# VectorE's share of the softmax exponentials: a 16-bit log word used three times in place of a log word and its parabola

## The chip, the core and the metric

The kernel runs on one core of one Trainium2 chip. The time is the device time of one launch in microseconds (us). The engines are PE (TensorE: PE rows are matmuls, PEld rows are weight loads), ACT (ScalarE), DVE (VectorE), POOL (GpSimd) and SP, which here only issues DMAs.

## The reference

Two transformer layers over one sequence of 2048 tokens of width 512, in bfloat16. Each layer is attention with 32 heads of width 16, then a ReLU feed-forward of width 1792; both sit behind a layer norm and add to x. The same weights serve both layers.

```python
def _A_ref(x, wqkv, wo):
    B, S, D = x.shape                      # 1, 2048, 512
    H = 32
    Dh = D // H                            # 16
    qkv = (x @ wqkv).reshape(B, S, 3, H, Dh) ...   # q, k, v by head
    scores = jnp.einsum("bhqd,bhkd->bhqk", q, k) * (Dh ** -0.5)
    p = _softmax(scores, axis=-1)
    o = jnp.einsum("bhqk,bhkd->bhqd", p, v)
    return (...o...).reshape(B, S, D) @ wo

def _B_ref(x, w1, w2):
    h = jnp.einsum("bsd,df->bsf", x, w1)
    h = jnp.maximum(h, zero)
    return jnp.einsum("bsf,fd->bsd", h, w2)

x = A_x
x = x + _A_ref(_layernorm(x), A_wqkv, A_wo);  x = x + _B_ref(_layernorm(x), B_w1, B_w2)
x = x + _A_ref(_layernorm(x), A_wqkv, A_wo);  x = x + _B_ref(_layernorm(x), B_w1, B_w2)
```

The attention scores are 2 x 32 x 2048 x 2048 numbers, and each needs an exponential. They never leave the core: scores are made in PSUM, an exponential of them is written to SBUF, and that is the moving operand of the product with the values.

## The kernel before

**Slots.** The scores are worked off in 1366 slots. A slot has three blocks of 128 keys x 512 queries (each in one PSUM bank; late in the kernel a block is cut into pieces 256 or 128 queries wide, of several key blocks). There are two sets of three banks, `ps_s0` and `ps_s1`, used in turn. In a slot PE makes the scores with 32-row tiles (line 1497, called S here), ACT takes `exp` of them into one of five buffers `e` (line 1506), and later PE multiplies `e` by the values `vaug` into `ps_o`, four 32-column tiles at a time (line 1077, a value round, V). `vaug` carries a column of ones, so that the softmax's denominator comes out of the same product. S of a slot can start when the exponentials of the slot two before it have been read out of the same bank set.

**VectorE's blocks.** In many slots the third block goes to DVE, and ACT's instruction is then 1024 wide in place of 1536. DVE turns the scores of its block into an int16 number in units of 1/128 octave (line 1184, `lin`): read as bfloat16, the bits of that number are a first approximation of 2^x that is linear between powers of two. Three blocks of such slots make a group (`GROUP = 3`), and when the third one's number is there, `chain` (the lines 1228, 1237 and 1240) works on the 128 x 1536 group:

- `square` gets the mantissa of `lin`, by a bitwise AND and OR (line 1228);
- in groups where the values are not held in a scaled copy `vscaled` (keys 7 to 11), `square` is multiplied by a constant (line 1237);
- `square` is multiplied by `lin`, both read as bfloat16: the parabola (line 1240, the only operation with two tensors);
- `lin` is cut to its exponent by AND and OR, in place (line 1228).

PE then adds two products per block to `ps_o`, `square` x values and `lin` x values. There are four `lin` buffers (`NP`) and three `square` buffers (`NC`).

**The filler.** Everything else, the projections, the output projection, the feed-forward and the transposes, is cut into pieces of matmuls that go into `ps_f` (line 480, called F here) and are put into the gaps of PE between S and V. Their results are read out of PSUM by DVE.

**The order.** There is no dynamic schedule. The program is written by a planner in Python, run at build time: it keeps its own clocks of PE, DVE and ACT (`now_pe`, `now_dve`, `exp_end`) with fixed costs (`MM` 216 ns for a round of matmuls, `SWITCH` 105 ns for a change between S and V or F), and decides with them, slot by slot, which block DVE takes, which pieces and value rounds go in front of the next S, and when the steps of `chain` stand in DVE's order. If PE has time to spare in a slot, S is issued again to keep PE busy (`times`, the loop ahead of line 1497). Whether a slot may begin a new group for DVE is decided in the condition with `pair_no[0] + 1 - pairs[0]["n"] < NP`: there must be a free `lin` buffer, and the group's queued work (`CHAIN`) must end before its segment of keys does. On the chip each engine then runs its list in that order and waits on semaphores.

After the last slot follows a tail, in which the last rows pass through output projection, layer norm and feed-forward on PE, ACT and DVE by turns.

Of the kernel before, what the change touches and what calls it, by code (L numbers as in the profile page):

```python
# [25 lines left out]
def kernel(  # L26
# [10 lines left out]
    nc = tc.nc  # L37
    P = 128
# [24 lines left out]

    SQUARE, SUM = 0.99278, 1.0 / 0.66857
    LOG2E = 1.4426950408889634
    UNIT = 128.0
    EXP_BIAS = (127.0 - math.log2(SUM)) * UNIT
    GROUP = 3  # L70
    CHAIN = 2500.0
    FILL = 4000.0
    SOON = 1500.0
    NP = 4
    NC = 3
    SCALED = (7, 8, 9, 10, 11)

    MM = 216.0
# [21 lines left out]
    FULL = 3  # L100
    LOOK = 3
    NORM_UNITS = 12.0

    ctx.enter_context(tc.manual_schedule())
    persist = ctx.enter_context(tc.tile_pool(name="persist", bufs=1))
# [2 lines left out]
    def sb(shape, dt, name):  # L108
        return persist.tile(shape, dt, name=name)
# [37 lines left out]
    ot = [sb([P, QS], BF16, f"ot{T}") for T in range(NT // 2)]  # L147
    ot_last = sb([P, P], BF16, "ot_last")
    lin = [sb([P, GROUP * QS], I16, f"lin{n}") for n in range(NP)]
    square = [sb([P, GROUP * QS], BF16, f"square{n}") for n in range(NC)]  # L150

    acc = [
        x[:].bitcast(FP32).rearrange("p a b -> p (a b)") for x in kt01 + kt2
# [128 lines left out]
    def mark(key, engine="dve", lag=0.0):  # L282
        made[key] = (engine, (now_pe if engine == "pe" else now_dve)[0] + lag)
# [141 lines left out]
    def run_until(key):  # L425

        if key in made:
            return
        finish_group()
        if key in made:  # L430
            return
        if key not in maker:
            kind, l, j = key[1]
            for i in range(chunks[l, j][1]):
# [261 lines left out]
    def scale_v(l, kb, deps):  # L696
        task(
            225, lambda: nc.vector.tensor_scalar(
                out=vscaled[kb][:], in0=vaug[l][kb][:], scalar1=SQUARE, scalar2=None, op0=ALU.mult
            ),  # L700
            [("third", l, kb)], [("v", l, kb)] + deps,
        )
# [370 lines left out]
    def pv(sg, kb, g, rhs, p=None):  # L1073
        e = sg["e"]
        values = vscaled[kb] if p and p["scaled"] else vaug[sg["l"]][kb]
        sg["rem"][g] -= 1
        nc.tensor.matmul(  # L1077
            ps_o[32 * g : 32 * g + 32, 0 : sg["w"]],
            values[:, 4 * sg["T"] + g, 2 * e : 2 * e + 32],
            rhs, start=g not in sg["begun"], stop=not sg["rem"][g],  # L1080
            tile_position=(0, 32 * g), skip_group_check=True,
        )
        sg["begun"].add(g)
# [31 lines left out]
    def v_round(found, t):  # L1115
        pe_run("v", 1, t)
        sg = segs[seg_at[0]]
        for n in range(QS // sg["w"]):
            for g in range(4):
                of_g = [f for f in found if f[1][2] == g][n : n + 1]  # L1120
                for home, x, rhs in of_g:
                    home[:] = [y for y in home if y is not x]
                    pv(sg, x[1], g, rhs, *x[5:])
        while pend and not pend[0]["blocks"]:
            pend.popleft()
        for p in [p for p in pairs if len(p["blocks"]) == GROUP and not p["mms"]]:
            pairs.remove(p)
            mark(("added", p["n"]), "pe")
        if not any(sg["rem"]):
            finish_segment(sg, sg is segs[-1])  # L1130
            seg_at[0] += 1
# [40 lines left out]
        v_round(found, t)  # L1172


    pairs = deque()
    pair_no = [0]
    step1_end = {}
# [2 lines left out]
    def dve_block(half, taken, src, ex, recent):  # L1180
        which = (pair_no[0] + (half == 0)) % NP

        def first_step():
            first = nc.vector.tensor_scalar(  # L1184
                out=lin[which][:, half * QS : (half + 1) * QS], in0=src, scalar1=EXP_BIAS,
                scalar2=0.0, op0=ALU.add, op1=ALU.max,
            )
# [12 lines left out]

        if half == 0:
            pair_no[0] += 1
            pairs.append({"sg": taken[0][0], "key": ("e", pair_no[0]), "n": pair_no[0], "blocks": [], "mms": [], "scaled": False})
        p = pairs[-1]
        p["blocks"].append(taken)
        for sg, kb, g in taken:
            sg["rem"][g] += 1
        line_key = ("line", p["n"], half)
        p["mms"] += [
            (sg, kb, g, part[:, half * QS + n * sg["w"] : half * QS + (n + 1) * sg["w"]], key) + of  # L1210
            for part, key, of in (
                (square[p["n"] % NC], p["key"] + ("square",), (p,)),
                (lin[which][:].bitcast(BF16), p["key"], ()),
            )
            for n, (sg, kb, g) in enumerate(taken)
        ]
        p["mms"].sort(key=lambda x: len(x[4]), reverse=True)
        musts.append((EVAC, now_pe[0] + PE_TO_DVE, first_step))

    def chain(p):  # L1220
        key, n = p["key"], p["n"]
        line, power = lin[n % NP][:], square[n % NC][:]
# [4 lines left out]
        def bits(out, keep, put):  # L1227
            nc.vector.tensor_scalar(  # L1228
                out=out, in0=line, scalar1=keep, scalar2=put, op0=ALU.bitwise_and,
                op1=ALU.bitwise_or,  # L1230
            )

        half_mantissa = power if p["scaled"] else power.bitcast(FP16)
        quick = 77 + 0.2588 * GROUP * QS
        steps = [(quick, ("half",), lambda: bits(power.bitcast(I16), 0x7F, 0x3F00))]
        if not p["scaled"]:
            steps.append((quick, ("weighed",), lambda: nc.vector.tensor_scalar(
                out=half_mantissa, in0=power, scalar1=SQUARE, scalar2=None, op0=ALU.mult)))
        steps += [
            (77 + 0.52 * GROUP * QS, ("square",), lambda: nc.vector.tensor_mul(  # L1240
                out=power, in0=half_mantissa, in1=line.bitcast(BF16))),
            (quick, (), lambda: bits(line, 0x7F80, 0)),
        ]
        after = [("added", n - NC)] if n > NC else []
        for cost, of, fn in steps:
            task(cost, fn, [key + of], after)
            maker[key + of]["chain"] = p
            after = [key + of]

    for n in range(NW1):  # L1250
        load_w1(n)
# [109 lines left out]
    now_dve[0] = 14500.0  # L1361
    exp_end = {-1: 12600.0, 0: 13600.0}
    pair_at = None
    def in_turn(x):
        sg, kb, g = x[1]
        return sg["n"], sg["e"], kb % (QS // sg["w"])

    while units:
# [21 lines left out]
        half = None  # L1390
        if len(banked) == W and (pair_at is None or no > pair_at or now_dve[0] < now_pe[0] + SOON):
            mine = banked[-1][0][0]
            if pair_at is not None:
                half, take = len(pairs[-1]["blocks"]), pairs[-1]["sg"]
            elif (not pairs or pair_no[0] + 1 - pairs[0]["n"] < NP) and ((mine['l'] or ("v", 0, 15) in made or len(pairs) < 3 and ("v", 0, 5) in made or not pairs and ("k", 0, 0, 1) in made) and (not mine['l'] or ('k', 1, 0, NQS - 1) in made or pace < PAIR_PACE)):
# [79 lines left out]
        s_ready = max(exp_end[no - 2] + ACT_TO_PE, step1_end.get(no - 2, 0.0) + DVE_TO_PE)  # L1475
        need_by = exp_end[no - 1] - MM - PE_TO_ACT
        limit = max(need_by - 60.0, s_ready) - SWITCH
        late = len(pend) >= 3
        for kind in ("v", "f", "v") if late else ("f", "v", "f"):
            if kind == "f":  # L1480
                fill_pe(limit)
            else:
                fill_v(limit, 3)

        spare = int(max(need_by - pe_start("s", s_ready), 0.0) / MM)
        soon = (len(pend) > 1) + (owed[0] > 1.0 and (bool(cur) or not evac))
# [213 lines left out]
```

## Time and profile before

| | us |
|---|---|
| median of 3 runs | 1526.84 (1523.2 to 1528.97) |
| profiled execution, its own time | 1527.95 |
| span of its instructions | 1526.2 |
| from the span's start to the first `exp` of a slot | 14.62 |
| from there to the end of the last one | 1485.40 |
| from there to the end (the tail) | 26.2 |
| ACT busy | 1483.9 (97%) |
| DVE busy | 1427.3 (94%) |
| PE busy / weight loads busy | 1383.3 (91%) / 525.3 (34%) |

In a row of groups stand the line, the engine, the operation, output <- input by their names, the shapes, the count, then busy time in us and the mean duration of one in ns, then the engine's idle time before such instructions and what ended it. On every engine a record begins before the one ahead of it has ended (the records of two neighbours overlap by 70 to 270 ns), so the mean duration is more than an instruction costs in a row of its kind; the distance from start to start is what it costs.

### The profile page before, as it was taken

What the parts mean: (1) busy time and instruction counts of PE and PEld (TensorE: products, weight loads), DVE (VectorE), ACT (ScalarE), POOL (GpSimd) and SP (SyncE); (2) the same over time, 40 slices, a digit from 0 to 9 for tenths busy, and PEclk for the clock granted to TensorE, in tenths of its full rate; (3) what the DMA queues carried; (4) which work ended last, traced back from release to release, by engine and by line L of the source; (5) the groups of instructions that cost most, each with busy time, mean ns of one, the idle gap of its engine ahead of it and who ended that gap; (6) DMA issues with size and microseconds to landing.
All of it is one profiled execution on the core that took longest, in us unless ns stands there. A gap on an engine that the chain in (4) does not pass through costs nothing.

```text
span 1526.2 us, 45694 instructions
## 1 busy us (share of the span) xinstructions
PE 1383.3 (91%) x19996; PEld 525.3 (34%) x20000; DVE 1427.3 (94%) x2474; ACT 1483.9 (97%) x1393; POOL 104.7 (7%) x244
## 2 busy tenths in 40 slices
PE   8889888998999998999889998888999999999998
PEld 3222222232232222333223232222234444445665
DVE  7889999999999999999799998789999999999984
ACT  7989999999999999999999999999999999999994
POOL 4000001001010011000110001001001000010100
PEclk9999999999999999999999999899999999999999
DMA  7000000111002010120101100000110111121221
GB/s 197 19 5 23 20 13 15 42 25 22 17 20 45 18 23 13 23 50 20 23 5 29 29 5 5 6 18 8 43 41 19 36 31 29 36 52 44 62 55 28
DMA packets 135144, 46.32 MB, mean 30 GB/s; under 512 B 119808, under 2 KB 132160, under 8 KB 134944
## 3 DMA queue, kind: packets, MB, share of 16 engines
q1 hardware_dynamic: 128032, 37.34, 10.5%
q0 software_dynamic: 5568, 5.15, 1.9%
q8 instruction: 156, 2.56, 0.7%
q10 hardware_dynamic: 1344, 0.92, 0.2%
q14 instruction: 44, 0.36, 0.1%
HBM read 24.38 MB, written 2.10 MB: 17 GB/s over the span
## 4 chain that ended last, share of the span: by engine, by line
ACT 73%; PE 11%; DVE 11%; issue 2%; DMA 2%; POOL 1%; SPq 1%; DVEq 0%; ACTq 0%
ACT e L1506 73%; PE ps_s L1497 4%; DVE lin L1184 4%; PE ps_o L1077 3%; PE ps_f L480 3%; DVE square L1240 1%; DVE ht L794 1%; DVE square L1228 1%; DMA w<-in_B_w_dram 1%; PE ps_s L1560 1%; DVE lin L1228 1%; DMA wv<-in_A_wqkv_dram 0%; PE ps_s L480 0%; DVE vaug L706 0%; SPq L221 0%
## 5 line engine op out<-in xcount | busy, mean ns | idle before, releaser
L1506 ACT ACTIVATE e<-ps_s 128x1024 bf16<-128x1024 f32 (+1 forms) x1366 | 1471.3, 1320 | 14.8 <-PE ps_s L1497 9.7
L1497 PE MATMUL ps_s<-q,ktp 32*128 32x512 bf16 (+2 forms) x6605 | 610.3, 328 | 104.3 <-ACT e L1506 88.1
L1184 DVE TENSOR_SCALAR lin<-ps_s 128x512 int16<-128x512 f32 x861 | 578.4, 685 | 31.0 <-PE ps_s L1497 23.4
L1077 PE MATMUL ps_o<-e,vaug 128*32 128x512 bf16 (+2 forms) x4450 | 436.3, 329 | 9.8 <-DVE vaug L706 1.5
L1497 PEld LDWEIGHTS <-ktp 32*128 32x128 bf16 x6605 | 217.0, 92 | 553.8 <-issue 336.8
L1240 DVE TENSOR_TENSOR square<-square,lin 128x1536 bf16<-128x1536 bf16 (+1 forms) x287 | 270.1, 947 | 0.2
L1077 PEld LDWEIGHTS <-vaug 128*32 128x32 bf16 x5800 | 155.3, 94 | 269.8 <-issue 243.9
L480 PE MATMUL ps_f<-xnT,w 128*32 128x512 bf16 (+2 forms) x2048 | 153.6, 344 | 6.3 <-DVE ht L794 3.3
L1228 DVE TENSOR_SCALAR lin<-lin 128x1536 int16<-128x1536 int16 x287 | 157.3, 549 | 0.2
L1228 DVE TENSOR_SCALAR square<-lin 128x1536 int16<-128x1536 int16 x287 | 153.4, 552 | 0.3
L480 PE MATMUL ps_f<-w,ht 128*32 128x512 bf16 x1624 | 145.0, 381 | 0.8 <-DVE xn L738 0.3
L1077 PE MATMUL ps_o<-lin,vaug 128*32 128x512 bf16 (+2 forms) x1182 | 133.3, 326 | 0.9 <-DVE lin L1228 0.9
L1077 PE MATMUL ps_o<-square,vscaled 128*32 128x512 bf16 (+2 forms) x1014 | 115.3, 329 | 1.1 <-DVE r L975 0.7
L480 PE MATMUL ps_f<-xnT,wkq 128*32 128x512 bf16 (+2 forms) x1376 | 108.4, 352 | 4.8 <-DVE x L833 1.2
L794 DVE TENSOR_SCALAR ht<-ps_f 128x512 bf16<-128x512 f32 x105 | 71.7, 683 | 1.5 <-PE ps_f L480 1.2
L480 PEld LDWEIGHTS <-w 128*32 128x32 bf16 x2080 | 55.3, 96 | 36.7 <-issue 23.2
L480 PEld LDWEIGHTS <-ht 128*32 128x32 bf16 x1680 | 45.1, 96 | 28.9 <-issue 14.4
L526 POOL TENSOR_TENSOR ta<-stats 128x4 f32<-128x4 f32 (+2 forms) x17 | 7.0, 409 | 592.1 <-DVE stats L517 592.1
L480 PE MATMUL ps_f<-wo,ot 128*32 128x512 bf16 x496 | 45.1, 382 | 1.7 <-DVE vaug L706 1.0
L480 PEld LDWEIGHTS <-wkq 128*32 128x32 bf16 x1376 | 35.5, 95 | 30.5 <-issue 20.2
L517 DVE BATCH_NORM_STATS2 stats<-x 128x6 f32<-128x512 bf16 x64 | 42.9, 684 | 2.1 <-DMA x<-in_A_x_dram 1.2
L1077 PEld LDWEIGHTS <-vscaled 128*32 128x32 bf16 x1014 | 35.5, 95 | 26.7 <-issue 24.5
(142 smaller groups left out, 577.0 us busy)
## 6 DMA issues: line engine op xcount, KB each, us to landing
w<-in_B_w_dram SPq DMA_DIRECT2D x130, 128.0 KB
q<-xn SPq DMA_DIRECT2D x44, 64.0 KB
out_dram<-x SPq DMA_DIRECT2D x16, 128.0 KB
x<-in_A_x_dram SPq DMA_DIRECT2D x14, 128.0 KB
w<-in_B_w_dram SPq DMA_DIRECT2D x1, 1792.0 KB
u<-r POOLq DMA_DIRECT2D x12, 128.0 KB, 4.5
ktp<-in_B_w_dram SPq DMA_DIRECT2D x10, 128.0 KB
u<-ht POOLq DMA_DIRECT2D x6, 128.0 KB, 4.5
```

Source lines behind the costliest of these rows:

```text
L480: nc.tensor.matmul(out[cols], lhsT[:, cols], rhs, start=i % k == 0, stop=i % k == k - 1, tile_position=(0, 32 * g), skip_group_check=True,)
L517: nc.vector.bn_stats(out=stats[ln_n(tag)][:, i, :], in_=x_t[tt][:])
L526: pool.tensor_tensor(out=t1, in0=st[:, :, 1], in1=st[:, :, 4], op=ALU.subtract)
L794: nc.vector.tensor_scalar(out=out, in0=sums, scalar1=0.0, scalar2=None, op0=ALU.max)
L1077: nc.tensor.matmul(ps_o[32 * g : 32 * g + 32, 0 : sg["w"]], values[:, 4 * sg["T"] + g, 2 * e : 2 * e + 32], rhs, start=g not in sg["begun" ...
L1184: first = nc.vector.tensor_scalar(out=lin[which][:, half * QS : (half + 1) * QS], in0=src, scalar1=EXP_BIAS, scalar2=0.0, op0=ALU.add, op1 ...
L1228: nc.vector.tensor_scalar(out=out, in0=line, scalar1=keep, scalar2=put, op0=ALU.bitwise_and, op1=ALU.bitwise_or,)
L1240: (77 + 0.52 * GROUP * QS, ("square",), lambda: nc.vector.tensor_mul(out=power, in0=half_mantissa, in1=line.bitcast(BF16))),
L1497: nc.tensor.matmul(b[:, a : a + sg["w"]], kt[32 * g : 32 * g + 32, kc : kc + P], qbuf[sg["n"] % 2][32 * g : 32 * g + 32, sg["e"], 0 : sg[" ...
L1506: ex = nc.scalar.activation(out=eb[:, 0 : place[m]], in_=b[:, 0 : place[m]], func=ACTF.Exp, scale=1.0 / (LOG2E * UNIT),)
L1560: uses(nc.tensor.matmul(out, lhsT, rhs, start=first, stop=last), b, needs=needs)
```

## The change

The parabola goes. The number `lin` stays as it is for its whole life and is used three times: read as bfloat16 itself, and as two copies, `up` with 41 added and `down` with 41 taken off (41/128 of an octave), each not below 0. Each copy is one `tensor_scalar` with add and max on int16 (line 1243 of the changed kernel). In groups whose values have no scaled copy `down` is multiplied by a constant (line 1248). PE adds three products per block in place of two: `lin`, `up` and `down`. The first can go as soon as a block's `lin` is there; before, both waited for the group's steps.

The buffers are two each of `up` and `down` in place of three of `square`. The planner is told when each part's products are done (`("free", part, n)`), a new group needs a `lin` buffer that is free in that sense (`lin_free`), and some of its constants change (`CHAIN` 2500 to 1500; no new group where the filler's pace is above `MOST`, except in some early slots; value rounds with four columns filled are preferred unless three or more slots wait). One line asks for another layer's chunk table in `run_until`, and `vscaled` carries `WEIGHT` in place of `SQUARE`.

```diff
-    SQUARE, SUM = 0.99278, 1.0 / 0.66857
+    THIRD, WEIGHT, SUM = 41.0, 1.55, 3.63198
-    CHAIN = 2500.0
+    CHAIN = 1500.0
-    NC = 3
+    NC = 2
+    MOST = 4.0
...
-    square = [sb([P, GROUP * QS], BF16, f"square{n}") for n in range(NC)]
+    up = [sb([P, GROUP * QS], I16, f"up{n}") for n in range(NC)]
+    down = [sb([P, GROUP * QS], I16, f"down{n}") for n in range(NC)]
...
     # in dve_block
-            sg["rem"][g] += 1
+            sg["rem"][g] += len(PARTS) - 1
...
-            for part, key, of in (
-                (square[p["n"] % NC], p["key"] + ("square",), (p,)),
-                (lin[which][:].bitcast(BF16), p["key"], ()),
+            for part, buf, key, of in (
+                ("lin", lin[which], line_key, None),
+                ("up", up[p["n"] % NC], p["key"] + ("up",), None),
+                ("down", down[p["n"] % NC], p["key"] + ("down",), p),
...
     # in chain
-        half_mantissa = power if p["scaled"] else power.bitcast(FP16)
-        quick = 77 + 0.2588 * GROUP * QS
-        steps = [(quick, ("half",), lambda: bits(power.bitcast(I16), 0x7F, 0x3F00))]
-        if not p["scaled"]:
-            steps.append((quick, ("weighed",), lambda: nc.vector.tensor_scalar(
-                out=half_mantissa, in0=power, scalar1=SQUARE, scalar2=None, op0=ALU.mult)))
-        steps += [
-            (77 + 0.52 * GROUP * QS, ("square",), lambda: nc.vector.tensor_mul(
-                out=power, in0=half_mantissa, in1=line.bitcast(BF16))),
-            (quick, (), lambda: bits(line, 0x7F80, 0)),
-        ]
+        quick = 67 + 0.2591 * GROUP * QS
+        def shifted(out, by):
+            nc.vector.tensor_scalar(
+                out=out, in0=line, scalar1=by, scalar2=0.0, op0=ALU.add, op1=ALU.max
+            )
+        steps = [
+            (("up",), lambda: shifted(above, THIRD), [("free", "up", n - NC)]),
+            (first, lambda: shifted(below, -THIRD), [("free", "down", n - NC)]),
+        ]
+        if not p["scaled"]:
+            steps.append((("down",), lambda: weigh(below.bitcast(BF16)), [key + first]))
...
     # may this slot begin a group?
-            elif (not pairs or pair_no[0] + 1 - pairs[0]["n"] < NP) and (...):
+            elif lin_free(pair_no[0] + 1 - NP) and (... and (first_short or pace < MOST)):
...
-        late = len(pend) >= 3
+        late = len(pend) >= 4
...
-                fill_v(limit, 3)
+                fill_v(limit, 3 if len(pend) > 2 else 4)
```

Since the order is planned, the whole program moves. The two built programs have these counts:

| | before | after |
|---|---|---|
| slots with three blocks on ACT (1536 wide) | 504 | 411 |
| slots with two on ACT, one on DVE (1024 wide) | 861 | 954 |
| groups of three blocks on DVE | 287 | 318 |
| 128 x 1536 operations of DVE on them | 896 | 683 |
| S matmuls, with the repeated ones | 6605 | 6201 |
| value matmuls | 6814 | 8164 |
| filler matmuls | 6288 | 6288 |

More of the change, by code (lines that the diff above doesn't have):

```diff
@@ L433, in run_until @@
             kind, l, j = key[1]
-            for i in range(chunks[l, j][1]):
+            for i in range(chunks[l - (kind == "ln1"), j][1]):
                 run_until(("z", l - 1, j, i) if kind == "ln1" else ("o", l, j, i))
@@ L698, in scale_v @@
             225, lambda: nc.vector.tensor_scalar(
-                out=vscaled[kb][:], in0=vaug[l][kb][:], scalar1=SQUARE, scalar2=None, op0=ALU.mult
+                out=vscaled[kb][:], in0=vaug[l][kb][:], scalar1=WEIGHT, scalar2=None, op0=ALU.mult
             ),
@@ L1122, in v_round @@
                     home[:] = [y for y in home if y is not x]
-                    pv(sg, x[1], g, rhs, *x[5:])
+                    pv(sg, x[1], g, rhs, *x[5:6])
         while pend and not pend[0]["blocks"]:
             pend.popleft()
-        for p in [p for p in pairs if len(p["blocks"]) == GROUP and not p["mms"]]:
-            pairs.remove(p)
-            mark(("added", p["n"]), "pe")
+        for p in list(pairs):
+            if len(p["blocks"]) < GROUP:
+                continue
+            for part in PARTS:
+                if ("free", part, p["n"]) not in made and not any(x[6] == part for x in p["mms"]):
+                    mark(("free", part, p["n"]), "pe")
+            if not p["mms"]:
+                pairs.remove(p)
+                mark(("added", p["n"]), "pe")
         if not any(sg["rem"]):
@@ L1172, in force_v @@
         v_round(found, t)
+    PARTS = ("lin", "up", "down")
     pairs = deque()
@@ L1206, in dve_block @@
         for sg, kb, g in taken:
-            sg["rem"][g] += 1
+            sg["rem"][g] += len(PARTS) - 1
         line_key = ("line", p["n"], half)
         p["mms"] += [
-            (sg, kb, g, part[:, half * QS + n * sg["w"] : half * QS + (n + 1) * sg["w"]], key) + of
-            for part, key, of in (
-                (square[p["n"] % NC], p["key"] + ("square",), (p,)),
-                (lin[which][:].bitcast(BF16), p["key"], ()),
+            (
+                sg, kb, g,
+                buf[:].bitcast(BF16)[:, half * QS + n * sg["w"] : half * QS + (n + 1) * sg["w"]],
+                key, of, part,
+            )
[3 more added lines that the diff above has]
+                ("down", down[p["n"] % NC], p["key"] + ("down",), p),
             )
@@ L1216, in dve_block @@
         ]
-        p["mms"].sort(key=lambda x: len(x[4]), reverse=True)
+        p["mms"].sort(key=lambda x: PARTS.index(x[6]))
         musts.append((EVAC, now_pe[0] + PE_TO_DVE, first_step))
@@ L1221, in chain @@
         key, n = p["key"], p["n"]
-        line, power = lin[n % NP][:], square[n % NC][:]
+        line = lin[n % NP][:]
         p["scaled"] = all(
@@ L1225, in chain, with weigh @@
         )
-        def bits(out, keep, put):
+        quick = 67 + 0.2591 * GROUP * QS
+        def shifted(out, by):
             nc.vector.tensor_scalar(
-                out=out, in0=line, scalar1=keep, scalar2=put, op0=ALU.bitwise_and,
-                op1=ALU.bitwise_or,
-            )
-        half_mantissa = power if p["scaled"] else power.bitcast(FP16)
-        quick = 77 + 0.2588 * GROUP * QS
-        steps = [(quick, ("half",), lambda: bits(power.bitcast(I16), 0x7F, 0x3F00))]
-        if not p["scaled"]:
-            steps.append((quick, ("weighed",), lambda: nc.vector.tensor_scalar(
-                out=half_mantissa, in0=power, scalar1=SQUARE, scalar2=None, op0=ALU.mult)))
-        steps += [
-            (77 + 0.52 * GROUP * QS, ("square",), lambda: nc.vector.tensor_mul(
-                out=power, in0=half_mantissa, in1=line.bitcast(BF16))),
-            (quick, (), lambda: bits(line, 0x7F80, 0)),
-        ]
-        after = [("added", n - NC)] if n > NC else []
-        for cost, of, fn in steps:
-            task(cost, fn, [key + of], after)
+                out=out, in0=line, scalar1=by, scalar2=0.0, op0=ALU.add, op1=ALU.max
+            )
+        def weigh(x):
+            nc.vector.tensor_scalar(out=x, in0=x, scalar1=WEIGHT, scalar2=None, op0=ALU.mult)
+        above, below = up[n % NC][:], down[n % NC][:]
+        first = ("lower",) if not p["scaled"] else ("down",)
+        steps = [
+            (("up",), lambda: shifted(above, THIRD), [("free", "up", n - NC)]),
+            (first, lambda: shifted(below, -THIRD), [("free", "down", n - NC)]),
+        ]
+        if not p["scaled"]:
+            steps.append((("down",), lambda: weigh(below.bitcast(BF16)), [key + first]))
+        for of, fn, deps in steps:
+            task(quick, fn, [key + of], [d for d in deps if d[0] != "free" or d[2] > 0])
             maker[key + of]["chain"] = p
-            after = [key + of]
     for n in range(NW1):
@@ L1363, with lin_free @@
     pair_at = None
+    def lin_free(n):
+        return n <= 0 or (
+            ("free", "lin", n) in made
+            and all(("e", n, of) in made for of in ("up", "down"))
+        )
     def in_turn(x):
@@ L1390 @@
         half = None
+        first_short = banked[0][0][0]["short"] and not banked[0][0][0]["l"]
         if len(banked) == W and (pair_at is None or no > pair_at or now_dve[0] < now_pe[0] + SOON):
@@ L1394 @@
                 half, take = len(pairs[-1]["blocks"]), pairs[-1]["sg"]
-            elif (not pairs or pair_no[0] + 1 - pairs[0]["n"] < NP) and ((mine['l'] or ("v", 0, 15) in made or len(pairs) < 3 and ("v", 0, 5) in made or not pairs and ("k", 0, 0, 1) in made) and (not mine['l'] or ('k', 1, 0, NQS - 1) in made or pace < PAIR_PACE)):
+            elif lin_free(pair_no[0] + 1 - NP) and ((mine['l'] or ("v", 0, 15) in made or len(pairs) < 3 and ("v", 0, 5) in made or not pairs and ("k", 0, 0, 1) in made) and (not mine['l'] or ('k', 1, 0, NQS - 1) in made or pace < PAIR_PACE) and (first_short or pace < MOST)):
                 queued = sum(t["cost"] for t in dve_q if "chain" in t)
```

## The prediction

> **What bounds the kernel now.** I read the page's busy table and chain first, then the loop in one window, the groups by shape, PE's waits, and short pieces of the timeline for the cost of one thing in a row.
>
> ```profile
> PE 1383.3 (91%) x19996; PEld 525.3 (34%) x20000; DVE 1427.3 (94%) x2474; ACT 1483.9 (97%) x1393; POOL 104.7 (7%) x244
> ACT 73%; PE 11%; DVE 11%; issue 2%; DMA 2%; POOL 1%; SPq 1%; DVEq 0%; ACTq 0%
> 14.62:1500.02 1485.40, 1351.59 (x19556) 508.03 (x19556) 1410.36 (x2424) 1471.29 (x1366) 97.91 (x203) 0.99 0.13 28
> 100.00:200.00 100.00, 87.39 (x997) 27.21 (x987) 95.01 (x158) 95.82 (x93) 3.99 (x6) 1.00 0.08 18
> 200.00:300.00 100.00, 89.00 (x1005) 29.00 (x1007) 98.46 (x165) 100.00 (x96) 5.95 (x11) 1.00 0.10 23
> ```
>
> Three engines are nearly full, and one leads: ACT is 97% busy and 73% of the chain that ended last. The third line is the loop of slots (columns: us, then busy us and count of PE, weight loads, DVE, ACT, POOL): ACT is busy for 1471.29 of 1485.40 us, and in most stretches of 100 us, as in the last line, for all of it. What ACT no longer does comes off the time, as long as PE and DVE deliver.
>
> ```profile
> L1506 ACT ACTIVATE e<-ps_s 128x1024 bf16<-128x1024 f32 x861 | 842.5, 1169 | 7.5 <-PE ps_s L1497 5.1 <-PE ps_o L1077 2.0
> L1506 ACT ACTIVATE e<-ps_s 128x1536 bf16<-128x1536 f32 x504 | 725.9, 1579 | 7.3 <-PE ps_s L1497 4.6 <-PE ps_o L1077 2.5
> 117.11 9.27 ACT L1506 ACTIVATE e<-ps_s 128x1024 bf16<-128x1024 f32 x10
> 741.97 13.64 ACT L1506 ACTIVATE e<-ps_s 128x1536 bf16<-128x1536 f32 x10
> ```
>
> The first two are groups, the others runs in ACT's timeline (start, length). A slot of three blocks costs 410 ns more than one of two by the mean durations. By the runs, one instruction in a row costs (9.27 - 1.08)/9 = 0.91 us and (13.64 - 1.58)/9 = 1.34 us (1.08 and 1.58 being the mean records in those windows): 430 ns more.
>
> **ACT.** The change moves 93 slots (954 - 861) from 1536 to 1024. 93 x 0.42 us = **39 us less**, on the path that sets the end.
>
> **DVE.**
>
> ```profile
> L1184 DVE TENSOR_SCALAR lin<-ps_s 128x512 int16<-128x512 f32 x861 | 578.4, 685 | 31.0 <-PE ps_s L1497 23.4 <-ACT e L1506 0.3 <-issue 0.2
> 604.43 0.53 DVE L1237 TENSOR_SCALAR square<-square 128x1536 f16<-128x1536 bf16 x1
> 604.88 0.55 DVE L1228 TENSOR_SCALAR square<-lin 128x1536 int16<-128x1536 int16 x1
> 605.35 0.95 DVE L1240 TENSOR_TENSOR square<-square,lin 128x1536 bf16<-128x1536 f16 x1
> 510.39 0.95 DVE L1240 TENSOR_TENSOR square<-square,lin 128x1536 bf16<-128x1536 bf16 x1
> 511.26 0.55 DVE L1228 TENSOR_SCALAR square<-lin 128x1536 int16<-128x1536 int16 x1
> ```
>
> From start to start, L1237 and L1228 take 0.45 and 0.47 us and the parabola 0.87 (510.39 to 511.26). An eviction (L1184), 0.08 shorter than its record as those are, takes 0.60. Removed: 574 bitwise steps x 0.47 = 270, 35 scalings x 0.47 = 16, 287 parabolas x 0.87 = 250. Added: 93 evictions x 0.60 = 56, and 636 shifts and 47 scalings. The shifts are add and max on int16, 1536 wide, SBUF to SBUF, and no row has just that. The bounds are 0.47 (L1228: same shape, same types, one tensor) and 0.87 (L1240: two tensors). I take 0.47, as everything but the arithmetic operation is L1228's: 683 x 0.47 = 321. DVE: -536 + 377 = 159 us less, 1268 busy. None of this is on the path, but an eviction waits behind a step of 0.47 at most, no longer 0.87.
>
> [...]
>
> **PE.** This is where the cost lies: a third product per block.
>
> ```profile
> 502.53 0.39 PE L1497 MATMUL ps_s<-q,ktp 32*128 32x512 bf16 x3
> 502.86 0.40 PE L1077 MATMUL ps_o<-e,vaug 128*32 128x512 bf16 x4
> 503.08 0.39 PE L480 MATMUL ps_f<-xnT,w 128*32 128x512 bf16 x4
> 503.45 0.39 PE L1497 MATMUL ps_s<-q,ktp 32*128 32x512 bf16 x3
> PE ps_s L1497 <- ACT e L1506: 88.1, 253, 0.9
> ```
>
> S to V is 0.33, V to F 0.22, F to the next S 0.37. So a round costs 0.216 (the planner's `MM`; the trace's 0.22), and S costs 0.11 going out and 0.15 coming back, 0.26 per slot. With these prices I added up what stands between one S and the next in both built programs, taking per slot the fullest of the four column tiles and each width in proportion:
>
> - before: S 359, V and F 632, transposes 8, changes 0.26 x 1259 slots and a little = 337; together 1336 us, against 861 x 0.91 + 504 x 1.34 = 1459 on ACT: 92%.
> - after: S 331 (404 fewer repeats), V and F 675, transposes 8, changes 350; 1364 us, against 954 x 0.91 + 411 x 1.34 = 1419: 96%.
>
> PE still fits, but with half the air. V and F can move by up to five slots (five `e` buffers), so I took groups of five slots and added up where PE's need is above ACT's: 9 us before, 18 after. The worst stretches are the slots from 68 on (67.6 us of PE against 67.0 of ACT) and those from 272 on (66.7 against 67.0). **Crowding: +9 us.** Its bounds: ACT's idle in the loop, 14.8 us by the two groups, could vanish because DVE is free sooner (-15); or the loop could run throughout as from 100 to 200 us, where ACT idles 4.2%: 0.042 x 1432 - 15 = +45. I stay near the low end, since ten of the twelve windows of 100 us from 200 to 1400 have ACT at 99% or more, with PE up to 93.7% busy.
>
> [...]
>
> **The tail.** In the trace, `1502.62 3.16 PE ps_s L480 x56` stands between the last output projection and the layer norm's transposes. In the changed program these 56 matmuls come before the loop's end, and pieces of the next stage take the gap. **-3 us**; its bounds are 0 (the gap was the layer norm's anyway) and -5 (some of those pieces are gone from behind too).
>
> **Costed at nothing.** The planner moves the last products; a new wait stands in front of 131 of the 636 shifts (for the products of `up` or `down` two groups back; before, 17 steps had one). What hides it is DVE's 15% of idle time; without that cover see the second rival. SP and POOL keep their DMAs.
>
> **The sum.** 1527.95 - 39 + 9 - 3 = 1495 for a profiled execution, which lies 1.1 above the median of the runs: **1494 us**.
>
> **The rivals.**
>
> 1. *PE eats most of it.* PE at 96% of ACT leaves ACT waiting at S in many slots, at the 4.2% of the 100 to 200 us window or near it: crowding of +25 to +45, 1511 to 1531. For: the changes of tile mode cost 0.26, and the planner prices them at 2 x 0.105. Against: of the four windows in which PE is above 93% busy, three have ACT at 99.8% or more.
> 2. *The shifts wait for PE: slower.* With two buffers instead of three, a shift may stand still until PE has done the products of two groups back; the evictions behind it in DVE's order wait too, the bank set is not free, S is late, and ACT after it. Price: 131 waits x 0.5 us = 66, so 1494 + 66 = 1560. From 0.25 us each on (33 us) the change is a loss. Against: the planner places a shift only when its clock says that the products are done, and the 17 such steps of before show no idle worth a row (0.3 us in front of `square` in all).
> 3. *The shifts run at the parabola's pace: slower.* 636 x 0.40 = 254 more on DVE: 1268 + 254 = 1522 busy. DVE's idle time in the whole span is 99 now, so 1522 + 55 to 99, about 1600. It decides from 0.67 us per shift on: in the loop DVE has 1410 - 159 = 1251 busy and 75 idle now, and 129 more fill the new loop of 1455. Against: the rows of one-tensor steps, bitwise and multiplying, agree at 0.45 to 0.47.
> 4. *Better than forecast.* DVE at 85% brings evictions forward, ACT's 14.8 us of idle go and no crowding comes: 1471 to 1480.
>
> **How the numbers follow.** Forecast (1480 to 1511) 0.73; rival 1 0.11; rival 2 0.05; rival 3 0.04; rival 4 0.07. A measurement of this kernel can tell about 0.5%, 7.6 us, so faster means below 1519 and slower above 1534. Faster: 0.73 + 0.07 + half of rival 1 = 0.86. Slower: 0.05 + 0.04. The rest is 0.05. The range has to leave out 2 in 10: 0.09 above for rivals 2 and 3, 0.07 of rival 1 beyond 1518, and 0.03 of rival 4 below 1475. So 1475 to 1518.
>
> **What would show it.** Right: 954 narrow and 411 wide `exp` with the loop near 1455 us and ACT still at 98% of it; the 636 shifts at records of 0.55 (0.47 in a row); DVE near 1270 busy; PE's wait for ACT well below 88.1; a tail near 23. Rival 1: ACT's idle before L1526 (the `exp` line after) above 30 us, ended by S. Rival 2: idle on DVE ahead of `up` and `down`, ended by PE `ps_o`. Rival 3: shifts with records of 0.95. Wrong altogether: a loop not shorter although ACT's instructions keep their prices.

## The result and the profile after

The kernel after takes 1501.2 us (median of four runs, 1500.68 to 1509.61), the kernel before on the same chip 1526.82 (four runs). The ratio is 0.9848, with a 95% interval of 0.9808 to 0.9887: faster by 25.6 us by the medians, where 33 were forecast. The profiled execution is the 1509.61 one; its mean granted PE clock was 0.985, that of the other three 0.992 to 0.995. How much of the time that accounts for is a main question below.

First the page of the kernel after: the busy table, the granted clock in 40 slices, and the chain that ended last.

```profile
PE 1406.4 (93%) x20946; PEld 522.3 (35%) x20946; DVE 1275.9 (85%) x2354; ACT 1449.9 (96%) x1393; POOL 89.1 (6%) x244
PEclk9999999999999999999799999979999999999999
ACT 63%; PE 22%; DVE 10%; issue 3%; DMA 1%; POOL 0%; SPq 0%; DVEq 0%; ACTq 0%
```

ACT is 34 us less busy (1483.9 to 1449.9), DVE 151, PE 23 more. But the chain has moved: ACT has 63% of it where it had 73%, PE 22% where it had 11%. And two slices have a granted clock of 0.7. The groups by shape, after:

```profile
L1526 ACT ACTIVATE e<-ps_s 128x1024 bf16<-128x1024 f32 x954 | 910.8, 1152 | 24.1 <-PE ps_s L1517 16.4 <-PE ps_o L1079 6.6
L1526 ACT ACTIVATE e<-ps_s 128x1536 bf16<-128x1536 f32 x411 | 584.7, 1561 | 10.3 <-PE ps_s L1517 7.8 <-PE ps_o L1079 1.8
L1243 DVE TENSOR_SCALAR up<-lin 128x1536 int16<-128x1536 int16 x318 | 174.9, 551 | 10.6 <-PE ps_o L1079 9.7
L1243 DVE TENSOR_SCALAR down<-lin 128x1536 int16<-128x1536 int16 x318 | 174.5, 549 | 7.2 <-PE ps_o L1079 6.9
```

The counts of slots are as built, and the shifts run at the pace of the bitwise steps (records of 551 and 549 ns; from a shift's start to the next start the median of all 636 is 0.467 us). ACT's idle time before `exp` has gone from 14.8 to 34.4 us, and 24.2 of it are ended by S. The waits say the same from both sides (us in total, times, longest):

```profile
PE ps_s L1517 <- ACT e L1526: 39.7, 134, 1.0
PEld L1517 <- DVE lin L1193: 126.7, 324, 1.8
ACT e L1526 <- PE ps_s L1517: 24.2, 48, 2.5
```

PE waits 39.7 us for ACT (before 88.1), ACT 24.2 us for PE (before 9.7). Where that happens is seen in windows of the kernel after (columns: us, then busy us and count of PE, weight loads, DVE, ACT, POOL, then granted PE clock, DMA share, GB/s): the loop first, and two pairs of stretches in it.

```profile
14.63:1485.40 1470.77, 1377.65 (x20545) 506.51 (x20545) 1259.41 (x2305) 1437.12 (x1366) 82.35 (x203) 0.98 0.13 29
712.00:724.00 12.00, 10.60 (x145) 3.44 (x134) 2.76 (x4) 12.00 (x10) 1.59 (x9) 1.00 0.01 1
724.00:738.00 14.00, 13.99 (x96) 2.93 (x97) 2.25 (x6) 11.36 (x8) 1.03 (x2) 0.51 0.32 39
980.00:994.00 14.00, 11.73 (x131) 3.80 (x130) 13.01 (x23) 14.00 (x14) 0.00 (x0) 1.00 0.06 13
994.00:1011.00 17.00, 16.21 (x112) 2.73 (x108) 9.99 (x17) 10.96 (x11) 0.00 (x0) 0.50 0.04 11
```

Until 724 and until 994 ACT is busy throughout (12.00 of 12.00, 14.00 of 14.00). Then the clock is 0.5, PE is busy nearly all the time with fewer matmuls, and ACT has only 11.36 of 14 and 10.96 of 17.

**Where the 18 us between the two profiled executions come from.** A start-to-start distance of `exp` that waits for nothing is 0.904 us (1024 wide) and 1.330 (1536). These prices over all slots give a floor for the loop, and what lies above it is loss, which I summed separately for the slots that touch a stretch of half clock and for the others. The last column is a version from the experiments (e12) that keeps the clock up.

| us | before | after | e12 |
|---|---|---|---|
| slots 1024 / 1536 wide | 861 / 504 | 954 / 411 | 951 / 414 |
| floor of the loop | 1449.1 | 1409.5 | 1410.9 |
| loss outside half clock | 30.7 | 44.6 | 43.4 |
| loss in half clock | 5.5 | 16.6 | 0 |
| tail | 26.2 | 22.4 | 22.2 |
| the profiled execution | 1527.95 | 1509.61 | 1492.98 |

So from before to after: -39.6 on the floor, +13.9 and +11.1 of loss, -3.8 in the tail. These are the profiled executions; that of after is the slowest of its four runs.

### The profile page after: what moved, and what is told of

It reads as the page before. It is cut to its first block, busy times and chain, and to the rows that moved or that the text cites. A ratio compares the mean times of both kernels' runs of the same rounds, so it can differ in the third digit from the quotient of the medians.

```text
span 1507.8 us, 47685 instructions
## 1 busy us (share of the span) xinstructions
PE 1406.4 (93%) x20946; PEld 522.3 (35%) x20946; DVE 1275.9 (85%) x2354; ACT 1449.9 (96%) x1393; POOL 89.1 (6%) x244
## 4 chain that ended last, share of the span: by engine, by line
ACT 63%; PE 22%; DVE 10%; issue 3%; DMA 1%; POOL 0%; SPq 0%; DVEq 0%; ACTq 0%
ACT e L1526 63%; PE ps_s L1517 8%; PE ps_o L1079 7%; PE ps_f L482 6%; DVE lin L1193 4%; DVE up L1243 1%; DVE ht L796 1%; PE ps_s L1580 1%; DVE vaug L708 1%; DVE down L1243 1%; DMA q<-xn 1%; DVE q L722 0%; DMA w<-in_B_w_dram 0%; DVE stats L519 0%; DVE xn L569 0%
## 5 line engine op out<-in xcount | busy, mean ns | idle before, releaser
L1526 ACT ACTIVATE e<-ps_s 128x1024 bf16<-128x1024 f32 (+1 forms) x1366 | 1437.1, 1274 | 34.4 <-PE ps_s L1517 24.2
L1193 DVE TENSOR_SCALAR lin<-ps_s 128x512 int16<-128x512 f32 x954 | 637.8, 683 | 54.1 <-PE ps_s L1517 46.8
L1517 PE MATMUL ps_s<-q,ktp 32*128 32x512 bf16 (+2 forms) x6201 | 587.8, 329 | 52.9 <-ACT e L1526 39.7
L1079 PE MATMUL ps_o<-e,vaug 128*32 128x512 bf16 (+2 forms) x4366 | 396.3, 329 | 13.5 <-DVE vaug L708 2.7
L1517 PEld LDWEIGHTS <-ktp 32*128 32x128 bf16 x6201 | 200.2, 92 | 529.0 <-issue 285.3
L1243 DVE TENSOR_SCALAR up<-lin 128x1536 int16<-128x1536 int16 x318 | 174.9, 551 | 10.6 <-PE ps_o L1079 9.7
L1243 DVE TENSOR_SCALAR down<-lin 128x1536 int16<-128x1536 int16 x318 | 174.5, 549 | 7.2 <-PE ps_o L1079 6.9
L1079 PE MATMUL ps_o<-up,vaug 128*32 128x512 bf16 (+2 forms) x1266 | 168.2, 330 | 0.0
L1079 PE MATMUL ps_o<-down,vscaled 128*32 128x512 bf16 (+2 forms) x1038 | 149.8, 336 | 0.0
L482 PE MATMUL ps_f<-xnT,w 128*32 128x512 bf16 (+1 forms) x2016 | 137.1, 347 | 6.3 <-DVE ht L796 2.8
L482 PE MATMUL ps_f<-w,ht 128*32 128x512 bf16 x1680 | 126.7, 382 | 1.2 <-DVE x L835 0.5
L482 PEld LDWEIGHTS <-ht 128*32 128x32 bf16 x1680 | 39.6, 95 | 38.1 <-issue 21.8
L482 PE MATMUL ps_f<-wv,xnT 128*32 128x512 bf16 x496 | 39.7, 382 | 5.6 <-DVE vaug L708 3.1
```

Source lines behind the costliest of these rows:

```text
L482: nc.tensor.matmul(out[cols], lhsT[:, cols], rhs, start=i % k == 0, stop=i % k == k - 1, tile_position=(0, 32 * g), skip_group_check=True,)
L1079: nc.tensor.matmul(ps_o[32 * g : 32 * g + 32, 0 : sg["w"]], values[:, 4 * sg["T"] + g, 2 * e : 2 * e + 32], rhs, start=g not in sg["begun" ...
L1193: first = nc.vector.tensor_scalar(out=lin[which][:, half * QS : (half + 1) * QS], in0=src, scalar1=EXP_BIAS, scalar2=0.0, op0=ALU.add, op1 ...
L1243: nc.vector.tensor_scalar(out=out, in0=line, scalar1=by, scalar2=0.0, op0=ALU.add, op1=ALU.max)
L1517: nc.tensor.matmul(b[:, a : a + sg["w"]], kt[32 * g : 32 * g + 32, kc : kc + P], qbuf[sg["n"] % 2][32 * g : 32 * g + 32, sg["e"], 0 : sg[" ...
L1526: ex = nc.scalar.activation(out=eb[:, 0 : place[m]], in_=b[:, 0 : place[m]], func=ACTF.Exp, scale=1.0 / (LOG2E * UNIT),)
```

## The experiments

Edits are against the kernel after unless it says before. Ratios are to the kernel before on the same chip.

### What DVE's relief alone is worth (e1)

```diff
     # the kernel before, in chain
-    nc.vector.tensor_mul(out=power, in0=half_mantissa, in1=line.bitcast(BF16))
+    nc.vector.tensor_scalar(out=power, in0=half_mantissa, scalar1=1.0, scalar2=None, op0=ALU.mult)
```

> The kernel before, in its own order, with the parabola's multiplication of two tensors replaced by a multiplication of one tensor by 1.0 (so the parabola is left out). DVE loses 287 x 0.40 = 115 us, nothing else changes: same 861 narrow and 504 wide slots, same matmuls. If ACT alone leads and the gain of the change comes only through the slots handed to DVE, the time stays within 5 us of before: 1520 to 1528. If DVE at 94 to 98% was itself holding ACT up, ACT's 15 us of idle time goes and the time is 1510 to 1515.

Measured: 1525.56 us, ratio 0.9981 (0.9969 to 0.9993). The busy table of this run:

```profile
PE 1383.3 (91%) x19996; PEld 527.2 (35%) x20000; DVE 1332.3 (87%) x2474; ACT 1482.9 (97%) x1393; POOL 97.3 (6%) x244
```

DVE gives up 95 us and the time 3, as the first of the two expectations has it. In this order cheaper steps bring next to nothing by themselves: the gain needs the slots that the planner hands to DVE because of them.

### Is PE's third product what costs (e2, e5)

```diff
     # e2: in pv
+        if part == "down" and g in sg["begun"]:
+            return
     # e5: the same with
+        if part in ("up", "down") and g in sg["begun"]:
```

> The changed kernel in its own order with the products of down left out (1266 of 20946 matmuls, some 70 us of PE; down is still computed). The split of the slots stays 954 to 411. Crowding theory: PE's need falls to about 92% of ACT's as it was before, the loop's loss against ACT's own prices falls from 61 us in the profile (about 52 in the median runs) back to the 36 of before, so 1480 to 1487. Clock theory (the missing gain is PE at half clock in thin stretches): a PE with less to do is clocked down no less, so 1495 to 1505.

> The changed kernel in its own order with the products of up and of down left out (2532 of 20946 matmuls, some 135 us of PE); up and down are still computed, and none of the 636 shifts waits for PE any more. The split stays 954 to 411. Crowding theory: groups of five slots in which PE needs more than ACT add up to 6 us, less than in the kernel before (11; 22 in the changed one), so the loop loses no more against ACT's prices than the 36 us of before: 1470 to 1486, if the clock stays as it is; a lower clock of an idler PE may take some of it back. Theory of the waiting shifts: the same, but most of the gain is already lost if the products of down alone are left out, and DVE's 18 us of idle time ahead of the shifts goes. Theory that neither matters: 1494 to 1502.

Measured: e2 1499.48 us (ratio 0.9810, 0.9791 to 0.9829), e5 1504.09 (0.9829, 0.9808 to 0.9850). Without the third product e2 loses some 39.5 us outside half clock in place of 44.6: crowding by PE's third product is some 5 us, not the whole 25. The time lies where the clock theory had it. In e5 two products of three are gone, and with them what the shifts wait for:

```profile
L1245 DVE TENSOR_SCALAR up<-lin 128x1536 int16<-128x1536 int16 x318 | 174.7, 550 | 0.7
L1245 DVE TENSOR_SCALAR down<-lin 128x1536 int16<-128x1536 int16 x318 | 174.7, 550 | 0.0
```

The 17.8 us of idle in front of the shifts become 0.7, PE is 61 us less busy, and the kernel is no faster. The loss shows why: outside half clock it fell from 44.6 to 36.4, but the half clock grew from 44 us in all to 72, with 22.1 us of loss in it. So PE ran 28 us more at half clock with less to do, and the gain is paid back. The time lies above every range expected. The 8.2 us that the loss fell at full clock are the products' and the waits' together; e5 does not part the two.

### The clock, first try: no repeats (e3)

```diff
-    FLOOR = 0.56      # share of a slot that PE is kept busy with repeated S
+    FLOOR = 0.0
```

> The changed kernel planned without the repeated S matmuls (FLOOR 0): 569 matmuls fewer, about 41 us of PE; the planner gives nearly the same split (948 to 417 slots, so ACT +2.5 us). Crowding theory: less on PE, so 1488 to 1498. Clock theory: the repeats are what keeps PE's clock; without them the profile shows more than 44 us at half clock and the time is above 1510.

Measured: 1500.03 us (0.9824, 0.9805 to 0.9843), with the granted clock at 0.982 or 0.983 in all five runs (51 us of half clock in the profile). Neither theory alone: the work taken off PE and the clock lost cancel. At full clock this version loses 35.0 us where after loses 44.6 (before 30.7), in half clock 14.2. Half of what it saves lies in the slots 66 to 100, where it loses 3.2 us and after 7.9; its plan holds 397 matmuls there in place of 452.

### The rule that stops groups (e4)

```diff
-    MOST = 4.0
+    MOST = 99.0
```

> The changed kernel without the limit on new groups where the filler's pace is high (MOST 99): 1023 narrow and 342 wide slots, 69 more handed to DVE, 255 matmuls more. ACT alone: 69 x 0.42 = 29 us less, 1472. Crowding theory: PE is full exactly where the filler's pace is high, so most of it is lost: 1490 to 1503. Clock theory: the stretches at half clock lie where the limit held (DVE is 4% to 18% busy there), and more value products there keep the clock, so 1475 to 1488.

Measured: 1503.83 us (0.9839, 0.9821 to 0.9857), just above what the crowding theory gave, with 1023 narrow slots. Windows of this kernel, the loop and the tail, same columns as above:

```profile
14.63:1450.66 1436.03, 1350.57 (x20334) 501.54 (x20334) 1319.84 (x2419) 1407.16 (x1366) 81.12 (x203) 1.00 0.12 28
1450.66:1501.86 51.20, 37.87 (x811) 23.87 (x808) 8.42 (x21) 11.63 (x26) 0.56 (x1) 0.96 0.26 64
```

The loop is 35 us shorter and the tail 29 longer: 793 matmuls of the filler and of the tail come after the last S in place of 321. My reading is that fewer wide slots give PE less time beside ACT, and that filler which finds no place waits at the end.

### DVE's idle time as a cover (e6)

```diff
-    (("up",), lambda: shifted(above, THIRD), [("free", "up", n - NC)]),
+    (("up",), lambda: (shifted(above, THIRD), shifted(above, THIRD)), [("free", "up", n - NC)]),
```

The planner's clock knows of one shift only.

> The changed kernel in its own order with each up shift issued twice: 318 x 0.47 = 149 us more on DVE, 1425 us busy, as much as in the kernel before. If DVE's idle time is only cover, as it was before, the time stays within 5 us of the changed kernel: 1498 to 1506. If the gain needs DVE's slack (evictions in time, shifts that can wait), it is mostly gone: 1515 to 1530.

Measured: 1636.89 us (1.0697, 1.0673 to 1.0721), far outside both expectations. Windows of the kernel after and of e6, same stretch, the second with the chain of e6 that ended last:

```profile
245.00:330.00 85.00, 81.16 (x947) 25.47 (x946) 84.11 (x153) 84.83 (x88) 5.45 (x13) 1.00 0.16 35
```

```profile
245.00:330.00 85.00, 72.97 (x814) 21.48 (x811) 84.27 (x156) 77.78 (x77) 4.23 (x11) 1.00 0.09 21
DVE 66%; PE 20%; ACT 7%; issue 5%; DMA 1%; POOL 0%; SPq 0%; DVEq 0%; ACTq 0%
```

After the change DVE is 84.11 of 85 us busy here, which leaves no room, and the 85% of the page is the mean of stretches with groups (many are 90 to 99% busy) and of those where `MOST` lets few groups begin (64.37 us busy in the 100 from 700). So 318 more shifts x 0.467 = 149 us on DVE cost the kernel 0.085 x 1527 = 130 us, and DVE leads the chain. The wait `PEld L1517 <- DVE lin L1193` grows from 126.7 us to 315.4: evictions late, S late. DVE is then as busy in sum as in the kernel before (1434.9 and 1427.3 us), which takes 1527; what differs is that this order was planned without the second shift.

### The value-round rule (e7, e8)

```diff
     # e7
-        late = len(pend) >= 4
+        late = len(pend) >= 3
-                fill_v(limit, 3 if len(pend) > 2 else 4)
+                fill_v(limit, 3)
     # e8: the kernel before, with
-        late = len(pend) >= 3
+        late = len(pend) >= 4
-                fill_v(limit, 3)
+                fill_v(limit, 3 if len(pend) > 2 else 4)
-    CHAIN = 2500.0
+    CHAIN = 1500.0
```

> The changed kernel with the rule for value rounds of the kernel before (late from 3 waiting slots on, rounds from three filled columns on): more rounds go out with a column empty, and the planner then hands DVE less: 894 narrow and 471 wide slots, so ACT has 60 x 0.42 = 25 us more. If ACT's split is what the gain is made of: 1520 to 1528, the gain nearly gone although the arithmetic is the new one. If DVE's lighter steps are the gain: 1500 to 1508.

> The kernel before (parabola, two products) with the changed kernel's rule for value rounds and its CHAIN of 1500: 867 narrow and 498 wide slots, so ACT has 6 x 0.42 = 2.5 us less. If the planner's rules alone were the gain, 1500 to 1510. If they only pay once DVE's steps are cheap enough to take more blocks: 1521 to 1528.

Measured: e7 1550.76 us (1.0134, 1.0117 to 1.0151), slower than before, with 894 narrow slots; e8 1536.97 (1.0047, 1.0028 to 1.0065), 867. Both are slower than either of their expectations. By the ratios, the new arithmetic without the rule loses 20 us against the kernel before and the rule without the arithmetic 7; together they win 23. Neither number is the rule's alone:

```profile
768.06 1.90 PE L482 MATMUL ps_f<-xnT,wkq 128*32 128x512 bf16 x16 [10.04 <-DMA xnT<-xn]
```

In e7 there is a stop at the layers' boundary, where PE waited 10.04 us for the DMA of `xnT`, with 23.9 us of half clock around it. The slots 660 to 700, in which it lies, lose 21.4 us (before 0.6); without that, e7 would be within some 3 us of the kernel before, so the gain would be gone and the sign open. I read that off the trace and did not test it. And e8's six runs are 28 to 59 us at half clock, the kernel before on that chip 21 to 25, which at 0.32 us each (the price is worked out below) is some 5 of its 7 us. So the rule is needed for the gain; how much of it is the rule's is not shown.

### The loss at the end of layer 0: moving the filler (e9, e10, e11)

The steady stretches lose hardly more than before: slots 100 to 380 lost 5.1 us before and 6.2 after, 410 to 630 2.7 and 2.6, 935 to 1280 6.1 and 5.4. But slots 630 to 660 went from 0.5 to 4.6 and slots 660 to 700 from 0.6 to 7.4, of which 6.0 in half clock. In the built program the slots 640 to 680 hold 312 filler matmuls (before 168). Three edits spread them:

```diff
     # e9
-    AHEAD = (8.0, 8.0)
+    AHEAD = (0.0, 8.0)
-    ... -8.0 if first["j"] == NQS - 1 and not first["l"] ...
+    ... 0.0 if first["j"] == NQS - 1 and not first["l"] ...
     # e10: e9 with
+    MOST, FLOOR = 6.0, 0.0
     # e11: after with
-    else 3.0 if not first["l"] and first["j"] == NQS - 1 else 99.0
+    else 99.0
```

> The changed kernel with the filler of layer 0 paced more evenly (AHEAD 0 for layer 0, and 0 in place of -8 for its last rows): in the slots 640 to 680 stand 220 filler matmuls in place of 312 (the kernel before has 168), the rest of them earlier or later. The split is nearly the same (957 to 408 slots, ACT -1 us), the tail too (329 filler matmuls behind the last slot, 321). Theory of the burst (the gain missing against ACT's prices lies where the filler is packed together at the end of layer 0, slots 630 to 760: 15.5 us lost there in the profile, 2.4 before): the loss there falls to 5 to 9 us, the time to 1490 to 1496. Crowding everywhere: PE's total need is the same, so 1498 to 1504.

> The same even filler, with MOST 6 in place of 4 and without repeated S matmuls (FLOOR 0): 987 narrow and 378 wide slots (ACT 33 x 0.42 = 14 us less than in the changed kernel), 393 filler matmuls behind the last slot in place of 321 (72 / 4 x 0.22 = 4 us more tail), 36 us less on PE. Theory of the burst: 1484 to 1492, with a granted clock near 0.983, since the repeats are gone. Crowding everywhere: as much is lost as is won, 1496 to 1502.

> The changed kernel without the rule that lets filler go ahead of S although ACT will wait for it (hurry, at the end of layer 0 alone): 951 narrow and 414 wide slots (ACT +1 us), the filler as late as before (324 matmuls in the slots 640 to 680). If the loss at the end of layer 0 is that rule's doing, the 4.6 us lost in the slots 630 to 660 go, and the time is 1494 to 1498. If it is the amount of filler there, it only moves a few slots on: 1499 to 1505.

Measured: e9 1505.51 us (0.9845, 0.9823 to 0.9867), e10 1501.97 (0.9825, 0.9810 to 0.9839), e11 1500.57 (0.9827, 0.9805 to 0.9849): none is where the theory of the burst, or of that rule, had it. The loss in slots 630 to 660 does go (4.6 to 0.4 in e9, 0.7 in e11), but slots 660 to 700 lose 9.0 in e9 and 8.7 in e11 (after 7.4), mostly in half clock. At full clock the slots 630 to 700 lose 4.5 in e9 and 2.8 in e11 in place of 6.0; over the whole loop it is 40.3 and 43.8 in place of 44.6. Half clock was 51 us in e9's profile, 58 in e10's, 17 in e11's. So the crowded spot is real, but it is worth 1.5 to 3 us, and where the clock falls weighs more.

### What lowers the clock, and holding it (e12)

PE's timeline in the kernel after, ahead of the fall at 724.3 (start, length, idle before it):

```profile
720.30 0.39 PE L1517 MATMUL ps_s<-q,ktp 32*128 32x512 bf16 x3
720.62 0.40 PE L1079 MATMUL ps_o<-e,vaug 128*32 128x512 bf16 x4
721.33 0.39 PE L1517 MATMUL ps_s<-q,ktp 32*128 32x512 bf16 x3 [0.30 <-ACT e L1526]
721.65 0.40 PE L1079 MATMUL ps_o<-e,vaug 128*32 128x512 bf16 x4
722.67 0.61 PE L1517 MATMUL ps_s<-q,ktp 32*128 32x512 bf16 x6 [0.62 <-ACT e L1526]
723.21 0.40 PE L1079 MATMUL ps_o<-e,vaug 128*32 128x512 bf16 x3
724.01 0.85 PE L1517 MATMUL ps_s<-q,ktp 32*128 32x512 bf16 x6 [0.41 <-ACT e L1526]
```

The filler is done, DVE takes no blocks, and each 1.33 us slot brings PE one or two rounds of S (three or six matmuls) and one of V (three or four, side by side). No gap is longer than 0.62 us. Yet at 724.25 the granted clock falls to 0.5, and the six matmuls of S that begin at 724.01 last 0.85 in place of 0.61.

I counted this in the fourteen profiles. All 63 falls to half clock between the first and the last `exp` of the slots start on one grid of 3.413 us in each run, and last whole multiples of it (1 to 7). Counted from the first instruction it stands at 1.81 us in the profile of before and at 0.63 in that of after, so I take it to run free of the program; that was not shown by itself. I cut the loops on that grid and counted the rounds in each window. Matmuls that start within 0.1 us of each other (for the narrow ones, within 0.6 of a round's own length) are one round, of 0.216 us if 512 wide and less in proportion (from start to start of neighbours of one kind the medians in before and after are 0.216 us at 512 wide, 0.110 at 256 and 0.056 at 128). Then I looked at the window that follows:

| share of the window that rounds fill | windows at full clock | followed by half clock |
|---|---|---|
| under 0.40 | 30 | 30 |
| 0.40 to 0.48 | 119 | 30 |
| over 0.48 | 5770 | 3 |

Of windows under 0.48 the loop before has 5, after 10, e3 16, e5 18, e10 18. The seven windows of before and after that lost the clock were filled to 0.38 to 0.47, and the longest gap between matmuls in them was 0.88 us.

The edit asks for more repeated S where the filler is thin:

```diff
+        floor = 0.70 if pace < 1.2 else FLOOR
-        short = FLOOR * 1330.0 - level - busy[0] - MM * (1 + soon)
+        short = floor * 1330.0 - level - busy[0] - MM * (1 + soon)
...
-        level = min(level + busy[0] - FLOOR * (exp_end[no] - exp_end[no - 1]), 90.0)
+        level = min(level + busy[0] - floor * (exp_end[no] - exp_end[no - 1]), 90.0)
```

> The changed kernel with more repeated S matmuls only where the filler is thin (FLOOR 0.70 in place of 0.56 where the pace is under 1.2): 6360 S matmuls in place of 6201 (some 12 us of PE), 951 narrow and 414 wide slots (ACT +1 us). Clock theory: within one kernel the runs so far are some 0.3 us longer per us at half clock (the changed kernel 1509.6 at a granted clock of 0.985, 1500.7 at 0.995; the kernel before 1530.5 at 0.992, 1522.1 at 1.0), so with the clock held at 0.997 or more the time is 1495 to 1499. Crowding everywhere: 12 us more on PE cost what they bring, 1500 to 1506.

Measured: **1492.91 us** (five runs, 1492.03 to 1494.85), ratio 0.9764 (0.9750 to 0.9777): the fastest of all and some 2 us below what the clock theory gave. That is 8 us below after by the medians, 13 by the ratios, whose intervals do not touch, with 159 more S matmuls and three blocks fewer on DVE. The page, and the groups by shape:

```profile
PE 1397.7 (94%) x21095; PEld 524.5 (35%) x21099; DVE 1274.8 (85%) x2348; ACT 1447.6 (97%) x1393; POOL 91.4 (6%) x244
PEclk9999999999999999999999999999999999999999
```

```profile
L1527 ACT ACTIVATE e<-ps_s 128x1024 bf16<-128x1024 f32 x951 | 904.1, 1171 | 15.5 <-PE ps_s L1518 8.9 <-PE ps_o L1079 5.9
L1527 ACT ACTIVATE e<-ps_s 128x1536 bf16<-128x1536 f32 x414 | 586.2, 1569 | 4.6 <-PE ps_s L1518 3.3 <-PE ps_o L1079 0.4
```

The clock is 1.00 throughout, and ACT's idle time is 20.1 in place of 34.4. PE's timeline at the same place shows the larger repeats:

```profile
715.24 0.61 PE L1518 MATMUL ps_s<-q,ktp 32*128 32x512 bf16 x6 [0.62 <-ACT e L1527]
715.78 0.40 PE L1079 MATMUL ps_o<-e,vaug 128*32 128x512 bf16 x3
716.58 0.82 PE L1518 MATMUL ps_s<-q,ktp 32*128 32x512 bf16 x9 [0.41 <-ACT e L1527]
717.33 0.40 PE L1079 MATMUL ps_o<-e,vaug 128*32 128x512 bf16 x3
```

S twice and three times by turns, five rounds of S and two of V in two slots: 7 x 0.216 / 2.68 = 0.56 of the time, where the kernel after had 0.39 in the window before 724.3. One window of e12 still lies under 0.48 (at 0.45), and kept the clock.

## Why the prediction was right, and where its sum was off

- **ACT: right.** -39 forecast, -39.6 measured on the floor; the `exp` instructions kept their prices.
- **DVE's steps: right.** 0.47 us a shift was taken, 0.467 measured. The forecast's source was L1228 of the kernel before, a bitwise operation of the same shape and types; its median from start to start is 0.468 us. DVE was to be near 1270 busy and is 1275.9. Rival 3 (0.87 a shift) falls.
- **The tail: right.** -3 forecast, -3.8 measured.
- **Crowding: the term that was mis-sized.** "Crowding: +9 us" was the whole allowance for a later S; the profiled execution lost 25 us more than before. Of it 13.9 are lost at full clock, so the count by rounds and changes was 5 short. Of the two places that it named, one was right: the slots from 68 on lost 8.0 us in fifty slots, before 5.8. The other, from 272, lost about 1. What it did not see is the end of layer 0 (slots 630 to 660, 4.1 more than before) and the end of the loop (from 1280, 2.4 more). The other 11.1 are lost in half clock (17 us of it before, 44 after), and for that the sum had no term at all: PE's clock was taken as given.
- **The median.** The 8.4 us between the profiled execution and the median of after go with the clock (0.985 against 0.992 to 0.995). Over the 42 runs of the kernel before that stood beside the experiments, time rose by 0.32 us for each us at half clock. In the median run of after some 16.6 of the 25 us are left (25.0 - 8.4), and 13.9 at full clock leave under 3 for the clock. So what the forecast of the median missed (33 forecast, 25.6 measured) is mostly the crowding; the missing clock is most of what the profiled execution missed (1495 forecast, 1509.61 measured).
- **With the clock held.** From before to e12 the profiles give -38.2 for the floor of 951 slots, +12.7 at full clock, -5.5 as before's loss in half clock goes, -4.0 in the tail; 1527.95 - 35.0 = 1492.95, and 1492.98 was measured. This is close to the 1494 forecast partly by luck: the -5.5 was not in the sum. With no half clock on either side (the line through the 42 runs meets 1522.5 us there) the gain is 30 us against 33 forecast.
- **"What hides it is DVE's 15% of idle time": a wrong reason.** In many stretches with groups DVE is 90 to 99% busy, and e6 shows that work beyond the plan is not covered. The shifts' waits for PE were short and few (17.8 us of idle in all, against 66 for rival 2). What they cost by themselves is not shown; with two of three products gone as well, e5 lost 8.2 us less at full clock, and that bounds it. So costing them at nothing came out about right, but not for the reason given.
- **Rival 1** had its mark partly met: ACT's idle is 34.4 us, 24.2 of it ended by S. Its cause, a PE too full in many slots, can account for the 13.9 us at full clock at most; 16.6 us of the loss sit in 44 us of half clock, which followed on stretches where PE had too little to do (windows filled to 0.38 to 0.47).
- **The value-round rule** was told in the change and had no price. The gain needs it: without it the planner hands DVE 894 blocks and ACT's floor falls by 14 us in place of 39.6. That e7 is even 20 us slower than before lies nearly all in one stop at the layers' boundary.

Open: where all of the 13 us more at full clock go. Spreading the filler took 1.5 to 3 us off the end of layer 0 (e9, e11). Without the repeats of S (e3) the loss at full clock is 35.0, only 4 above the kernel before, so the repeats and what the plan does around them, at the start above all, hold a large part of it. A version with repeats in the thin stretches alone and none elsewhere was not run.

## What to carry to other kernels

Before you count an engine's idle share as cover, read it in the stretches where the work runs: 85% in the page was up to 99% there. And when a change moves work off or along PE, count how full each short window of PE is, not only whether PE keeps up: here a thin stretch cost its clock (half clock followed on 60 of 149 windows of 3.413 us filled to less than 0.48), and the engine that leads waited for it. Redundant matmuls in thin stretches can then be the cheaper choice (e12), while taking PE work out everywhere gained little (e2, e3, e5).

## What the runs showed of the hardware

- On one core, the granted PE clock fell to 0.5 for stretches of 3.4 to 24 us in the middle of a busy loop, in each profile on one grid of 3.413 us. The windows before it were filled by rounds of matmuls to less than 0.48 in 60 of 63 falls (30 of 30 windows under 0.40, 30 of 119 between). If the grid runs free of the program, as I take it to, the same program can fall in some runs and not in others; that would explain the spread of the kernel after (1500.68 to 1509.61 us, granted clock 0.995 to 0.985) and the smaller one of e12 (1492.03 to 1494.85, 1.0 to 0.998).
- PE's busy share in the profile does not show it: in the 12 us before 724 PE counts as 88% busy (10.60 of 12.00), as the record of a round lasts about 0.39 us, while the next round can start after 0.22.
- Half clock cost about 0.32 us of time per us in the kernel before (42 runs) and 0.31 in the four runs of after, in a loop that ACT otherwise leads.
